# Delta rule with a cosine router: the triangular inverse in 16-row blocks, with a level of matrix products between two blocks

## The chip, the core and the metric

The kernel runs on one core of a Trainium2 chip. The metric is the device time of one execution in microseconds (us). The core has a TensorE for matrix products (PE in the profile, its weight loads PEld), a VectorE (DVE), a ScalarE (ACT), a GpSimd (POOL), and a SyncE (SP) from whose queue most transfers start. Each engine works through its own queue in order and waits for others by semaphores. Matrix products land in PSUM, from which DVE or ACT take them to SBUF.

## What is computed

Two stages, all in fp32. The first is a delta rule over 4 x 8 = 32 heads, 768 steps, head width 48:

```python
B, H, S, D = q.shape                       # 4, 8, 768, 48
k_n = k / (np.linalg.norm(k, axis=-1, keepdims=True) + 1e-06)
state = np.zeros((B, H, D, D), dtype=np.float32)
for t in range(S):
    kt, vt, bt = (k_n[:, :, t], v[:, :, t], beta[:, :, t, None])
    y[:, :, t] = np.einsum('bhd,bhde->bhe', q[:, :, t], state)
    v_old = np.einsum('bhde,bhd->bhe', state, kt)
    state = state + bt[:, :, :, None] * np.einsum('bhd,bhe->bhde', kt, vt - v_old)
```

The second takes y as 3072 tokens of 384 numbers, normalizes them, scores them against 8 experts, sends each token to its best expert (384 to 1024 to 384 with a relu between), and scales the result by the router's probability.

## The kernel before

The delta rule is done in chunks of C = 64 steps. Inside a chunk the steps depend on one another through a unit lower triangular 64 x 64 matrix for each head, which has to be inverted; between chunks only the 48 x 48 state is carried. The kernel has 12 chunks (index m) and splits the 32 heads in two halves (index i), so there are 24 **units**, n = 2m + i. The 128 partitions hold two batches' chunks of 64 steps.

**Groups.** Two chunks (four units) make a group g, six groups in all. `prepare(g)` (L429 to L585) makes what all four units need: it loads k (`planned_k`), forms norms (`square`, `total`, `roots`, `scales`), the scaled keys K (`keys`), turns them on TensorE (`transposes`, L316) and copies them out to KQ on ScalarE. `gram_diag` (L522) then multiplies keys with keys on TensorE for the two 32-row diagonal blocks of each 64 x 64 matrix. `to_lanes` (L553) is a VectorE transpose that brings all those 32 x 32 blocks into lanes: each of the 128 partitions then holds one whole block of 32 x 32 numbers (32 heads x 2 chunks x 2 blocks), in the 128 x 1024 tile X. `lower` (L558, L560, GpSimd) clears what is not below the diagonal.

**Substitution.** The loop of L563 inverts the 32 x 32 block in every partition at once on VectorE: for each j from 1 to 30 a `product` (L568) of a column and a row, (31 - j) x j numbers, and a `subtract` (L572) of it from the rows below. That is 60 dependent VectorE instructions a group. `from_lanes` (L580) transposes the result back to WT, and two ScalarE copies, `spread` (L584, in the trace L283 with W as output), write it into W: for every head a 64 x 64 matrix with the two inverted 32 x 32 diagonal blocks.

**Units.** `unit(n)` (L633) is the recurrence. For one unit: `old` (the state times the keys), `rest` (L677, VectorE, R = V minus that), `solve` (W times R), `y_out` (ScalarE), `fix` (the lower left 32 x 32 corner, Sx), `u_out`, `solve_again` (W again), `z_out`, `update`, `new_state` (L726, or L728 for the first chunk; VectorE). Two such chains, i = 0 and i = 1, run side by side. Each TensorE step is 16 matrix products of 48 to 64 rows and columns, which the trace shows as 32 rows (a fp32 product here is two rows). Beside the chain each unit needs `gram` (keys with keys and queries), `scores` (L659, M), `from_state`, `inside`, the output x and its transposes and router scores; `routing` for every four units; and values and queries are loaded, scaled and turned. `solve` of the first unit of a group cannot start before that group's W.

**Order.** The instructions of the whole first stage are recorded as tasks with an engine, an estimated cost and a due time (`plan.add`), and `Plan.order` lays them out once, before the launch, by a list schedule: of the tasks that are ready by its estimates an engine takes the one with the earliest due time. A due time is written relative to t0, the start of the group or unit, where a unit is given PERIOD = 7.5. The engines then follow that fixed order, whatever the true durations are. PSUM is four pairs of banks; a task with `take` needs a free pair, which its last reader releases.

Tiles X, WT and the k ring lie in the space of the first expert's weights (`w1_first`, `w2_first`), so the trace calls X, WT and the loaded k `w_first`. The weights are loaded there once they are no longer used. `early_tile` does two expert tiles beside the last units. Then comes the second stage (L1115 to L1362): lists of tokens, gathers, and products with 24 loads of 1.5 MB of weights.

## Time and profile before

| | us |
|---|---|
| median of 3 runs | 620.38 (618.40 to 622.43) |
| the profiled execution | 617.46 |
| its span, first to last instruction | 615.6 |
| first stage: first `solve` starts (PE, reads W) | 66.71 |
| first stage: last unit's `rest` (L677) | 315.53 |

In the profile a row of an engine is one instruction: start, duration, engine, line, operation, output and inputs, their shapes, and in brackets how long the engine was idle before it and which event ended that. "issue" means that nothing in the profile explains the wait. A table by windows gives the busy time of each engine in a stretch, with its count of instructions, and PEclk, the clock that TensorE was granted as a share of full speed. TensorE's rows overlap, and their ends are modelled.

The page's first part gives the engines' totals over the span: PE 516.1 us (84%), PEld 425.9, DVE 275.9 (45%), ACT 185.4, POOL 168.5. The 45% of VectorE is an average over two stages: of its 275.9 us, 224.9 lie in the first 300.

### The profile page before, as it was taken

Reading aid. Unit: us, or ns where it says so; the run is one execution under the profiler, and the core shown is the slowest. Engines: PE = TensorE matmul, PEld = TensorE weight load, DVE = VectorE, ACT = ScalarE, POOL = GpSimd, SP = SyncE. Lnnn points to the kernel's source line nnn. Section 1 sums busy time; section 2 is a strip of 40 time slices with the busy share of each in tenths; the row PEclk is TensorE's granted clock in tenths of the full one; section 3 lists DMA queues with packets and bytes.
Section 4 is the critical chain, followed back from the end, with each engine's and each line's share of the span. In section 5 each row is a group of like instructions: output and inputs, shape, how many; then the busy total and the mean of one; then the engine's idle time right before and its main releaser. Section 6 shows DMA issues by size and latency. Waiting matters only on the chain. (4 is left out here: it accounts for less than half of the span.)

```text
span 615.6 us, 21947 instructions
## 1 busy us (share of the span) xinstructions
PE 516.1 (84%) x9643; PEld 425.9 (69%) x9643; DVE 275.9 (45%) x778; ACT 185.4 (30%) x343; POOL 168.5 (27%) x228
## 2 busy tenths in 40 slices
PE   3573688688797878888899599999999999999990
PEld 3462577578686767777887577887767777777870
DVE  4798777777789877962325121111011221121000
ACT  2331534634635536555442020111001221110110
POOL 4433426064534132230212212331202211111100
PEclk9965678667879897998899799999999999999996
DMA  4444734543341340032201599997637666679300
GB/s 81 75 82 82 198 72 71 105 99 70 65 100 32 90 135 18 19 101 66 85 31 43 184 383 384 382 370 256 227 139 245 187 207 237 209 254 338 131 15 18
DMA packets 116334, 90.55 MB, mean 147 GB/s; under 512 B 83394, under 2 KB 105308, under 8 KB 116226
## 3 DMA queue, kind: packets, MB, share of 16 engines
q1 hardware_dynamic: 110722, 77.76, 42.7%
q0 software_dynamic: 4416, 11.06, 5.1%
q8 instruction: 80, 1.31, 0.9%
q10 hardware_dynamic: 1088, 0.20, 0.2%
q14 instruction: 28, 0.23, 0.1%
HBM read 77.06 MB, written 12.13 MB: 145 GB/s over the span
## 5 line engine op out<-in xcount | busy, mean ns | idle before, releaser
L1200 PEld LDWEIGHTS acc<-xTm,w 128*128 128x128 f32 x576 | 77.7, 191 | 5.8 <-issue 1.8
L1202 ACT ACTIVATE hT<-acc 128x512 f32<-128x512 f32 (+3 forms) x52 | 28.5, 548 | 175.2 <-PE acc L1200 175.2
L1200 PE MATMUL acc<-xTm,w 128*128 128x128 f32 (+3 forms) x576 | 80.3, 299 | 0.0
L1217 PE MATMUL acc<-w,hT 128*128 128x384 f32 (+2 forms) x272 | 78.9, 489 | 0.0
L572 DVE TENSOR_TENSOR w_first<-w_first,tmp 128x30 f32<-128x30 f32 (+9 forms) x180 | 69.0, 385 | 3.9
L568 DVE TENSOR_TENSOR tmp<-w_first 128x30 f32<-128x30 f32 (+9 forms) x180 | 66.7, 372 | 4.1
L280 PE MATMUL psum_pair<-KQ 48*32 48x64 f32 (+2 forms) x2304 | 50.0, 265 | 18.9 <-issue 9.2
L1230 POOL DMA_INDIRECT out_dram<-y,more_ids x22 | 21.7, 986 | 160.5 <-DVE y L1220 127.4
L1217 PEld LDWEIGHTS acc<-w,hT 128*128 128x128 f32 (+2 forms) x272 | 42.2, 176 | 30.3 <-issue 5.8
L1191 DVE COPY xTm<-acc 128x384 f32<-128x384 f32 (+3 forms) x26 | 12.6, 508 | 109.1 <-PE acc L1190 104.5
L280 PEld LDWEIGHTS psum_pair<-KQ 48*32 48x32 f32 (+1 forms) x2304 | 42.4, 135 | 24.4 <-issue 12.1
L1220 DVE TENSOR_SCALAR y<-acc,xg 128x384 f32<-128x384 f32 x20 | 12.4, 618 | 97.7 <-PE acc L1217 93.2
L1200 PEld LDWEIGHTS acc<-xTm,w_first 128*128 128x128 f32 x288 | 44.6, 200 | 3.7 <-DVE y L1227 0.6
L1200 PE MATMUL acc<-xTm,w_first 128*128 128x128 f32 (+3 forms) x288 | 46.8, 325 | 0.4 <-DVE xTm L1191 0.4
L1217 PE MATMUL acc<-w_first,hT 128*128 128x384 f32 (+2 forms) x176 | 44.2, 489 | 0.0
L280 PE MATMUL psum_pair<-S,KQ 48*64 48x64 f32 x1408 | 35.6, 244 | 9.9 <-issue 4.7
L280 PEld LDWEIGHTS psum_pair<-S,KQ 48*64 48x64 f32 x1408 | 30.5, 155 | 13.4 <-issue 6.3
L283 ACT ACTIVATE KQ<-psum_pair 128x1024 f32<-128x1024 f32 x24 | 24.4, 1022 | 43.5 <-PE psum_pair L316 33.7
L973 POOL DMA_INDIRECT idmap<-tokid,slots_i x24 | 24.1, 1005 | 42.3 <-DVE slots_i L949 22.8
L1217 PEld LDWEIGHTS acc<-w_first,hT 128*128 128x128 f32 (+2 forms) x176 | 23.1, 163 | 17.8 <-issue 4.5
L622 POOL TENSOR_TENSOR V<-v,sqb 128x384 f32<-128x384 f32 x24 | 20.9, 876 | 48.8 <-DVE R L677 22.0
L469 POOL TENSOR_TENSOR rt<-rn,half 128x32 f32<-128x32 f32 x4 | 22.0, 5488 | 30.2 <-DVE rn L454 30.2
(207 smaller groups left out, 766.2 us busy)
## 6 DMA issues: line engine op xcount, KB each, us to landing
w<-in_moe_w_dram SPq DMA_DIRECT2D x24, 1536.0 KB
w_first<-in_moe_w_dram SPq DMA_DIRECT2D x10, 1536.0 KB
q<-in_q_dram SPq DMA_DIRECT2D x96, 48.0 KB
v<-in_v_dram SPq DMA_DIRECT2D x48, 96.0 KB
w_first<-in_k_dram SPq DMA_DIRECT2D x88, 48.0 KB
x_dram<-XC SPq DMA_DIRECT2D x5, 800.0 KB
idmap<-space SPq DMA_DIRECT2D x1, 2048.0 KB
w_first<-in_moe_w_dram SPq DMA_DIRECT2D x6, 256.0 KB
```

Source lines behind the costliest of these rows:

```text
L280: nc.tensor.matmul(out_, lhsT=lhsT, rhs=rhs, start=start, stop=True, skip_group_check=True)
L283: nc.scalar.activation(out_, in_, ACT.Copy, scale=scale)
L469: nc.gpsimd.tensor_tensor(out=flat(rt, part), in0=flat(ss, part), in1=half[:, 0:w], op=ALU.pow)
L568: nc.vector.tensor_tensor(t, X[:, j + 1:, j:j + 1].broadcast_to([128, rows, j]), X[:, j:j + 1, 0:j].broadcast_to([128, rows, j]), op=ALU.mult)
L572: nc.vector.tensor_tensor(X[:, j + 1:, 0:j], X[:, j + 1:, 0:j], t, op=ALU.subtract)
L622: nc.gpsimd.tensor_tensor(buf("V", m)[:, i * 2 * NP * D:(i + 1) * 2 * NP * D].rearrange("p (jj j d) -> p jj j d", jj=2, d=D), buf("v", m)[ ...
L973: put = nc.gpsimd.indirect_dma_start(out=idmap[:, :], out_offset=bass.IndirectOffsetOnAxis(ap=slot_i[:, i:i + 1], axis=0), in_=K["tokid"][ ...
L1191: nc.vector.tensor_copy(t.xT[:, :, b * T:b * T + n], psX[:, :, 0:n])
L1200: nc.tensor.matmul(psH[:, i, :], lhsT=t.w1[:, j, (f + i) * 128:(f + i + 1) * 128], rhs=t.xT[:, j, 0:t.width], start=(j == 0), stop=(j == K ...
L1202: nc.scalar.activation(t.hT[:, f:f + k, 0:t.width], psH, ACT.Relu)
L1217: nc.tensor.matmul(psO[c:c + w, :], lhsT=t.hT[:, f, b * T + o:b * T + o + w], rhs=t.w2[:, f, :], start=(f < q), stop=(f >= NF - q))
L1230: nc.gpsimd.indirect_dma_start(out=out[:, :], out_offset=bass.IndirectOffsetOnAxis(ap=t.ids[b][0:n, 1:2], axis=0), in_=y[0:n, :], in_offse ...
```

## The change

Substitution now inverts 16 x 16 blocks instead of 32 x 32 ones. The 32 x 32 block of a partition is taken as two 16-row blocks (`blocks`, index e), which go through the loop side by side in the same instructions: j from 1 to 14, 28 instructions a group, each over 2 x (15 - j) x j numbers.

What connects the two 16-row blocks is then made by a **level** of products on TensorE. `rows_from_lanes` transposes the inverted first 16 rows (128 x 512) into WN, `from_lanes` clears one 16 x 16 corner (a memset on VectorE) and transposes the whole X to WT as before. Two ScalarE copies (`rows_spread`, 128 x 512 each, with the new masks `first` and `second`) write WN into W. `level_one` multiplies, for each of 32 places and both halves of the partitions, a 64 x 64 weight out of W with 16 columns of WT: 64 products, in two tasks. `level_one_out` (ScalarE, 128 x 512, mask `lo`) takes that to WN; `level_two` multiplies again, 64 products in two tasks; `merged` (VectorE, 128 x 512) adds the result into WT. Only then come the two `spread` copies of 128 x 1024 that were there before. The level holds one PSUM pair from its first product to `merged`.

All due times of the preparation are two units later (the k load -12 instead of -14 periods, and so on down to -5.4 instead of -7.2 for `gram_diag`); the level's own due time is L1 = -3.3 periods, where W had -1.8 before. X has one buffer instead of two, and W is cleared once at the start (GpSimd memsets of 128 x 2048, two of them). Nothing outside the first stage's preparation is edited; but as the schedule is laid out anew, the order of the instructions around it changes too.

```diff
--- before
+++ after
 HC = 32
+LC = 16
...
-    rings["X"], rings["WT"] = carved(2, [HC, HC], w2_flat), carved(3, [HC, HC], w2_flat)[2:]
-    buffers("tmp", 2, [(HC // 2) * (HC // 2)])
+    lanes = HC * HC + HC
+    rings["X"] = [w2_flat[:, 0:lanes]]
+    rings["WT"] = carved(1, [HC, HC], w2_flat[:, lanes:])
+    rings["WN"] = carved(1, [LC, HC], w2_flat[:, lanes + HC * HC:])
+    buffers("tmp", 2, [2 * (LC // 2) * (LC // 2)])
     buffers("W", 2, [HC, C])
...
+        nc.vector.tensor_scalar_mul(const("second", [128, 1]), nsec, -1.0)
+        nc.vector.tensor_scalar_mul(const("first", [128, 1]), K["nfirst"], -1.0)
+        sub = const("sub", [128, 1], I32)
+        nc.vector.tensor_single_scalar(sub, prow[:, 0:1], HC - 1, op=ALU.bitwise_and)
+        lo = const("lo", [128, 1])
+        nc.vector.tensor_copy(lo, sub)
+        nc.vector.tensor_single_scalar(lo, lo, float(LC), op=ALU.is_lt)
         for t in rings["Sx"]:
             nc.gpsimd.memset(t[:, :, 0:HC], 0.0)
+        for t in rings["W"]:
+            nc.gpsimd.memset(t, 0.0)
...
-            planned_k(m, t0 - 14 * PERIOD + (m % 2) * 2 * PERIOD if m > 1 else -200.0 + 0.5 * m)
+            planned_k(m, t0 - 12 * PERIOD + (m % 2) * 2 * PERIOD if m > 1 else -200.0 + 0.5 * m)
...
-        X = buf("X", g)
+        lane = buf("X", g)
+        X = lane[:, 0:HC * HC].rearrange("p (a b) -> p a b", a=HC)
+        blocks = lane.rearrange("p (e q) -> p e q", e=2)[:, :, 0:LC * HC].rearrange("p e (a b) -> p e a b", b=HC)
 
         def to_lanes():
             nc.vector.transpose(X, pair(("diag", g)).rearrange("p jj (x c) -> p c jj x", c=HC))
-        plan.add(*dve(1024), t0 - 6.5 * PERIOD, to_lanes, hold=g == 0, reads=[("psum", ("diag", g))],
+        plan.add(*dve(1024), t0 - 4.9 * PERIOD, to_lanes, hold=g == 0, reads=[("psum", ("diag", g))],
                  writes=[at("X", g), ("X_next", g % 2)])
 
         def lower():
             nc.gpsimd.affine_select(out=X, in_=X, compare_op=ALU.is_ge, fill=0.0, base=-1,
                                     pattern=[[1, HC], [-1, HC]], channel_multiplier=0)
-            nc.gpsimd.memset(X.rearrange("p a b -> p (a b)")[:, ::HC + 1], -1.0)
-        plan.add("POOL", 1.2, 0.1, t0 - 6.4 * PERIOD, lower, writes=[at("X", g)])
-
-        for j in range(1, HC - 1):
-            rows = HC - 1 - j
-            t = buf("tmp", j)[:, 0:rows * j].rearrange("p (a b) -> p a b", b=j)
+            nc.gpsimd.memset(lane[:, 0:HC * HC:HC + 1], -1.0)
+        plan.add("POOL", 1.2, 0.1, t0 - 4.8 * PERIOD, lower, writes=[at("X", g)])
+
+        for j in range(1, LC - 1):
+            rows = LC - 1 - j
+            t = buf("tmp", j)[:, 0:2 * rows * j].rearrange("p (e a b) -> p e a b", e=2, b=j)
 
             def product(j=j, rows=rows, t=t):
-                nc.vector.tensor_tensor(t, X[:, j + 1:, j:j + 1].broadcast_to([128, rows, j]),
-                                        X[:, j:j + 1, 0:j].broadcast_to([128, rows, j]), op=ALU.mult)
+                nc.vector.tensor_tensor(t, blocks[:, :, j + 1:LC, j:j + 1].broadcast_to([128, 2, rows, j]),
+                                        blocks[:, :, j:j + 1, 0:j].broadcast_to([128, 2, rows, j]), op=ALU.mult)
 
             def subtract(j=j, rows=rows, t=t):
-                nc.vector.tensor_tensor(X[:, j + 1:, 0:j], X[:, j + 1:, 0:j], t, op=ALU.subtract)
-            key = t0 - (6.0 - j * 4.0 / HC) * PERIOD
-            plan.add("DVE", rows * j / 960 + 0.085, 0.13, key, product, reads=[at("X", g)], writes=[at("tmp", j)], hold=g == 0)
-            plan.add("DVE", rows * j / 960 + 0.085, 0.13, key + 0.01, subtract, reads=[at("tmp", j)], writes=[at("X", g)], hold=g == 0)
-
-        WT, W = buf("WT", g), buf("W", g)
+                to = blocks[:, :, j + 1:LC, 0:j]
+                nc.vector.tensor_tensor(to, to, t, op=ALU.subtract)
+            key = t0 - (4.6 - j * 1.2 / LC) * PERIOD
+            plan.add("DVE", 2 * rows * j / 960 + 0.15, 0.1, key, product, reads=[at("X", g)], writes=[at("tmp", j)], hold=g == 0)
+            plan.add("DVE", 2 * rows * j / 960 + 0.15, 0.1, key + 0.01, subtract, reads=[at("tmp", j)], writes=[at("X", g)], hold=g == 0)
+
+        WT, WN, W = buf("WT", g), buf("WN", g), buf("W", g)
+        level = ("level", g)
+        L1 = t0 - 3.3 * PERIOD
+
+        def rows_from_lanes():
+            nc.vector.transpose(WN, X.rearrange("p a b -> p b a")[:, 0:LC])
 
         def from_lanes():
+            nc.vector.memset(X[:, LC:, 0:LC], 0.0)
             nc.vector.transpose(WT, X)
-        plan.add(*dve(1024), t0 - 1.9 * PERIOD, from_lanes, reads=[at("X", g)], writes=[at("WT", g), ("X_next", g % 2)])
+        plan.add(*dve(512), L1, rows_from_lanes, hold=g == 0, reads=[at("X", g)], writes=[at("WN", g)])
+        plan.add("DVE", 1.35, 0.17, L1 + 0.01, from_lanes, hold=g == 0, writes=[at("X", g), at("WT", g), ("X_next", g % 2)])
+        for b, name in enumerate(("first", "second")):
+            def rows_spread(b=b, name=name):
+                act_copy(W[:, :, b * HC:b * HC + LC], WN.rearrange("p r x -> p x r"), K[name])
+            plan.add(*act(512, True), L1 + 0.02, rows_spread, reads=[at("WN", g), "masks"], writes=[at("W", g) + (b,)])
+        half_x = [[jj * 16 + o * 8 + n for jj in range(2) for n in range(8)] for o in range(2)]
+
+        def level_one(xs):
+            def step():
+                p = pair(level)
+                for x in xs:
+                    for o in range(2):
+                        mm(p[HALF[o], 0, x * LC:(x + 1) * LC], W[HALF[o], x], WT[HALF[o], LC:, x])
+            return step
+
+        def level_one_out():
+            act_copy(WN.rearrange("p r x -> p (r x)"), pair(level)[:, 0], K["lo"])
+
+        def level_two(xs):
+            def step():
+                p, part = pair(level), WN.rearrange("p r x -> p (r x)")
+                for x in xs:
+                    for o in range(2):
+                        mm(p[HALF[o], 1, x * LC:(x + 1) * LC], W[HALF[o], x], part[HALF[o], x * LC:(x + 1) * LC])
+            return step
+
+        def merged():
+            to = WT[:, LC:].rearrange("p c x -> p x c")
+            nc.vector.scalar_tensor_tensor(out=to, in0=pair(level)[:, 1].rearrange("p (x c) -> p x c", c=LC),
+                                           scalar=K["lo"], in1=to, op0=ALU.mult, op1=ALU.add)
+        both = [at("W", g) + (0,), at("W", g) + (1,)]
+        for a in range(2):
+            plan.add(*pe(32, 0.0335), L1 + 0.03 + a * 0.01, level_one(half_x[a]), reads=both + [at("WT", g)],
+                     writes=[("psum", level)] if a else (), take=None if a else level)
+        plan.add(*act(512, True), L1 + 0.05, level_one_out, reads=[("psum", level), "masks"], writes=[at("WN", g)])
+        for a in range(2):
+            plan.add(*pe(32, 0.0335), L1 + 0.06 + a * 0.01, level_two(half_x[a]), reads=both + [at("WN", g)],
+                     writes=[("psum", level)])
+        plan.add(*dve(512), L1 + 0.08, merged, hold=g == 0, reads=[("psum", level), "masks"], writes=[at("WT", g)])
         for b, name in enumerate(("nfirst", "nsecond")):
             def spread(b=b, name=name):
                 act_copy(W[:, :, b * HC:(b + 1) * HC], WT.rearrange("p i x -> p x i"), K[name])
-            plan.add(*act(1024, True), t0 - 1.8 * PERIOD, spread, reads=[at("WT", g), "masks"], writes=[at("W", g) + (b,)])
+            plan.add(*act(1024, True), L1 + 0.1, spread, reads=[at("WT", g), "masks"], writes=[at("W", g) + (b,)])
 
...
-                         writes=["w2_first", ("X", 0), ("X", 1), ("WT", 0)])
+                         writes=["w2_first", ("X", 0), ("WT", 0), ("WN", 0)])
```

## The prediction

> **What bounds the kernel now.** I read the table by windows first, because the page averages two stages.
>
> ```profile
> core 0: us, PE busy (x) PEld busy (x) DVE busy (x) ACT busy (x) POOL busy (x), PEclk, DMA share, GB/s
> 0.00:66.00 66.00, 32.13 (x843) 27.19 (x843) 51.35 (x142) 19.63 (x26) 29.92 (x80) 0.76 0.45 80
> 66.00:134.00 68.00, 54.26 (x1657) 47.68 (x1661) 50.46 (x140) 31.52 (x55) 25.24 (x18) 0.73 0.51 114
> 134.00:250.00 116.00, 94.04 (x3506) 85.17 (x3496) 93.68 (x260) 57.91 (x101) 39.64 (x48) 0.87 0.32 72
> 250.00:275.00 25.00, 21.07 (x792) 19.26 (x785) 21.34 (x69) 11.91 (x27) 7.25 (x11) 1.00 0.15 44
> 275.00:300.00 25.00, 21.27 (x837) 19.36 (x829) 8.06 (x27) 14.79 (x29) 3.15 (x4) 0.93 0.24 79
> ```
>
> Up to 66 us, before any unit runs, VectorE is busy 78% and TensorE half idle. From 66 to 250 both are busy about 80%: VectorE 144 and TensorE 148 of 184 us. Past 275 the substitution is over, VectorE drops to a third, TensorE stays at 85%. So TensorE stands close behind VectorE. ScalarE at about half, the transfers and GpSimd are further off.
>
> Second, the groups of VectorE, for what the substitution costs:
>
> ```profile
> L572 DVE TENSOR_TENSOR w_first<-w_first,tmp 128x30 f32<-128x30 f32 (+9 forms) x180 | 69.0, 385 | 3.9
> L568 DVE TENSOR_TENSOR tmp<-w_first 128x30 f32<-128x30 f32 (+9 forms) x180 | 66.7, 372 | 4.1
> ```
>
> 135.7 us, half of all VectorE work: 22.6 us a group. Third, the timeline, for how it holds the units up (first the start, then units 2, 4, 5 and 23 at their `rest`, and the first products of unit 4):
>
> ```profile
> 32.73 0.13 DVE L568 TENSOR_TENSOR tmp<-w_first 128x30 f32<-128x30 f32 x1
> 60.66 0.19 DVE L572 TENSOR_TENSOR w_first<-w_first,tmp 128x30 f32<-128x30 f32 x1
> 62.64 2.07 ACT L283 ACTIVATE W<-w_first,nfirst 128x1024 f32<-128x1024 f32 x1 [7.14 <-DVE w_first L580]
> 90.28 0.55 DVE L677 TENSOR_TENSOR R<-V,psum_pair 128x384 f32<-128x384 f32 x1 [1.38 <-PE psum_pair L280]
> 110.47 0.54 DVE L677 TENSOR_TENSOR R<-V,psum_pair 128x384 f32<-128x384 f32 x1
> 116.51 1.13 PE L280 MATMUL psum_pair<-R,W 64*64 64x64 f32 x32 [1.96 <-ACT W L283]
> 134.02 0.56 DVE L677 TENSOR_TENSOR R<-V,psum_pair 128x384 f32<-128x384 f32 x1 [0.85 <-PE psum_pair L280]
> 315.53 0.56 DVE L677 TENSOR_TENSOR R<-V,psum_pair 128x384 f32<-128x384 f32 x1 [2.23 <-PE psum_pair L280]
> ```
>
> Group 0's substitution takes 28 us, and the first `solve` follows at 66.71. Unit 4's R is ready at 111.0, but its `solve` waits for group 1's W until 116.5. Units 5 to 23 then take (315.53 - 134.02) / 18 = 10.1 us each. With VectorE nearly free, units 18 to 22 take (302.25 - 269.65) / 4 = 8.15 us each.
>
> **VectorE.** Removed: 60 instructions a group. Added: 28 of 28 to 112 elements. The rows of L568 and L572 with 30, 58, 84 and 108 elements have means of 187 to 373 ns, together 264 ns, so 28 x 0.264 = 7.4 us instead of 22.6. Added too: a transpose of 128x512, half of L580's 1.24 us; a memset of 256 elements, 0.27 us as the one of L336; `merged`, between 0.68 us (L659, as large, also from PSUM) and 1.4 us (a strided copy of 1024 costs ScalarE 2.07 us where a plain one costs 1.02); I take 0.8. Net: 22.6 - 7.4 - 1.7 = 13.5 us a group, 81 us in all.
>
> **ScalarE.** Per group two `rows_spread` at half of 2.07 us and one copy of 128x512, 0.6 us between the rows for 384 (0.49) and 1024 (1.02): 2.7 us a group, 0.7 a unit. At half load there is room, but the chain's Y and U are queued behind the spreads, up to 2 us late once a group.
>
> **TensorE.** 128 products a group, 256 rows. Nearest rows: `solve`, also 64x64 weights, has 32 rows in 0.69 us at clock 1 and in 1.13 at the 0.61 of 108 to 131 us. That makes 5.5 us, or 9.0 cold. `gram_diag` with 128 rows in 1.53 us would make 3.1; the small beta products (142 rows in 5.55 us) 10.0. I take `solve` at full clock, 5.5 us a group or 1.4 us a unit, since the weights are the same and only the columns shrink; the ends are 0.8 and 2.5.
>
> The Trainium skill (TensorEngine Tiling, section Instruction Overhead) speaks against the change: a product with one column takes as long as one with 60, so tiling should not be taken from a dimension that is already small. By proportion to the columns (16 of 64) the level would cost 1.4 us a group, by the rule 5.5. The trace sides with the rule: router scores with 8 columns (6 rows in 0.84 us) cost as much a row as transposes with 128 (8 rows in 1.09).
>
> **The start.** No gain by my walk through the new queues. Substitution starts about 1 us later (GpSimd scales V, 1.62 us, before it clears X). In its middle stands `total` for chunk 3, whose ScalarE square now follows two Sx copies; these were at 38.8 and 40.1, and the first product of `gram` can start a little earlier, after the Q copy at 35.2: the square ends near 39.6, VectorE waits some 2.5 us. 28 instructions later it is 46 us. Transposes 2.2, spreads 2.1: 50. On TensorE, in front of the level, stand q of chunk 1 (its second half landed at 47.98), and between the four parts of the level the K transposes (up to 2 us each) and both `gram_diag` (1.5 to 2.6 each) of group 1: 10 to 15 us with the level. Then `merged`, Sx, and W's 4.1 us: first `solve` at 66 to 71 instead of 66.7. I take +2. The W memsets (4.6 us by the rate of L364) lie in GpSimd's idle time before the first K at 16.8.
>
> **Units 0 to 5.** Here the gain is clearest. Group 1's substitution, spread over 64 to 111 us before, needs a sixth of that; the queue of TensorE has unit 2's `old` ahead of group 2's diagonal products, where it stood behind them, and unit 5's first steps between those of units 4 and 6 rather than behind a whole unit and its routing. VectorE's longest remaining wait is for GpSimd's 5.5 us root, until about 79. From there unit 2's `rest` near 84 (before 90.3), unit 4's `solve` near 104 (116.5), unit 5's `rest` near 109 to 112 (134.0). Gain 22 to 25 us.
>
> **Units 5 to 23.** The pace is bounded by 8.15 + 1.4 = 9.55 us below (VectorE free, the level added) and 10.1 + 1.4 = 11.5 above (TensorE already the bound). What speaks for the middle: from 66 to 318 us TensorE was busy 208 of 252 us, the level adds 27, and 235 of 252 cannot be kept with waits for ScalarE and VectorE in the chain, unless rows get shorter. They can: at clock 1.00 a row cost 21.07 / 792 = 26.6 ns, over the whole stretch 28.5. I take 10.4. The last `rest`: 109 + 18 x 10.4 = 296 instead of 315.5: 19.5 us. (W's lateness: its first reader stands 19 to 30 tasks behind the level's last product in TensorE's queue, a unit and more, so I cost it at nothing; if not, see the second rival.)
>
> The skill on the clock gate (TensorE: Matmul & The Clock Gate, section What's actually happening) says that about 3.4 us of sustained work brings the full clock. The trace agrees only roughly: 0.73 over 66 to 134 us at 80% busy, but 1.00 over 250 to 275 at 84%. Going by the rule, all rows would shrink to the full clock's, and the pace would lie at the lower bound, 9.55.
>
> The second stage begins after the first and is unchanged. **Sum:** 617.5 - 19.5 = 598 us on the profiled execution's own time; that lies 2.9 us below the median of the runs, so 601.
>
> **Rivals.** (1) *VectorE was the only brake* (chance 0.14): pace at the lower bound, 9.55: last `rest` at 281, 34.5 us off, 586. For it: the stretch past 275; against: TensorE at 85% there already. (2) *W late, slower* (0.20): from the last substitution to W it took 6 us (60.85 to 66.65); now seven hand-overs through three queues, 15 us without any waiting (2.2 + 2.1 + 2.8 + 0.6 + 2.8 + 0.8 + 4.1), and the preparation comes two units later. TensorE's queue is in order, so a level that waits for ScalarE holds the units' steps behind it. If W's second half ends after R of the group's first unit, each group pays; at 8 us for five groups, 40 - 19.5 makes 641; the sign turns at about 4 us a group. Against: the place of its first reader. (3) *TensorE is the bound* (0.16): pace 11.5, last `rest` at 109 + 207 = 316: no change, 621. The forecast has 0.50, with its own range 590 to 613.
>
> **Chances.** About 1% (6 us) is what this measurement can tell from no change. Faster by more: nearly all of the forecast, rival 1, a little of the third: 0.64. Slower: rival 2 and a part of the third: 0.22. Same: 0.14. The range of 8 in 10 reaches from a little beyond rival 1 to half of rival 2: 579 to 630.
>
> **What would show it.** VectorE busy near 195 us; 128x512 copies of `rows_spread` near 1.04 us; the level's 64 rows near 1.4 us; first `solve` at 66 to 71; unit 5's `rest` near 110; 10.4 us a unit after it; TensorE over 88% busy from 110 us on. I am wrong if a wait of TensorE for ScalarE's W or WN shows more than 4 us a group, if the level's rows cost more than 30 ns each, or if the time gained by unit 5 is lost again by unit 23.

## The result and the profile after

The change makes the kernel slower: 685.58 us (676.88 to 688.85, four runs) against 621.12 (618.40 to 622.43) on the same chip, a ratio of 1.096 with a 95% interval of 1.090 to 1.103. The ratio counts only executions within 1.5% of the fastest of their kernel, so it is smaller than that of the medians (1.104), and the profiled execution, 688.62 us with a span of 686.9, is not among them; the profiles of prep_early and two_banks below, whose executions do count, show the same price of the level (77.4 and 77.0 us). The forecast was 601, its range 579 to 630.

| start of | before, us | forecast | after |
|---|---|---|---|
| first `solve` | 66.71 | 66 to 71 | 76.28 |
| unit 2's `rest` | 90.28 | 84 | 88.10 |
| unit 5's `rest` | 134.02 | 109 to 112 | 141.91 |
| last `rest` (unit 23) | 315.53 | 296 | 385.20 |
| pace of units 5 to 23, us a unit | 10.1 | 10.4 | 13.5 |

What comes after the last `rest` is as long as before, 686.9 - 385.2 = 301.7 us against 300.1. The whole loss lies in the first stage. Its windows, in the columns of the table before (length, busy time and count for each engine, granted clock, transfers):

```profile
0.00:66.00 66.00, 40.28 (x984) 36.46 (x984) 37.75 (x116) 17.48 (x25) 27.01 (x78) 0.71 0.51 105
66.00:142.00 76.00, 67.88 (x1903) 63.38 (x1904) 33.03 (x96) 36.59 (x59) 24.38 (x22) 0.69 0.33 62
142.00:250.00 108.00, 95.26 (x2955) 88.22 (x2956) 44.71 (x117) 45.67 (x77) 35.15 (x36) 0.73 0.29 62
250.00:300.00 50.00, 44.31 (x1352) 41.33 (x1349) 16.76 (x49) 21.45 (x35) 8.40 (x12) 0.77 0.24 63
300.00:385.00 85.00, 75.02 (x2354) 69.16 (x2358) 30.07 (x110) 37.28 (x80) 18.48 (x26) 0.87 0.17 52
```

VectorE did get lighter: 41% busy between 142 and 250 us, where it was 81% between 134 and 250. TensorE is 88 or 89% busy from 66 us on, and at a lower clock: 0.69 to 0.77 until 300 us, where before had 0.87 to 1.00 from 134 on. What filled it stands on the page in the costliest groups: the level, its products and the weight loads that overlap them (busy us, mean ns of a row):

```profile
L284 PE MATMUL psum_pair<-w_first,W 64*64 64x16 f32 x1536 | 77.1, 250 | 7.4 <-issue 4.2
L284 PEld LDWEIGHTS psum_pair<-w_first,W 64*64 64x64 f32 x1536 | 75.4, 200 | 10.6 <-issue 6.4
```

77.1 us for six groups is 12.85 us a group, 50 ns a row; the prediction had 5.5. The timeline shows two prices:

```profile
46.94 3.60 PE L284 MATMUL psum_pair<-w_first,W 64*64 64x16 f32 x64 [1.70 <-ACT KQ L287]
76.28 1.98 PE L284 MATMUL psum_pair<-V,W 64*64 64x64 f32 x64 [1.33 <-ACT W L287]
92.42 3.44 PE L284 MATMUL psum_pair<-w_first,W 64*64 64x16 f32 x62
141.91 0.55 DVE L738 TENSOR_TENSOR R<-V,psum_pair 128x384 f32<-128x384 f32 x1
213.40 2.04 PE L284 MATMUL psum_pair<-w_first,W 64*64 64x16 f32 x64 [0.29 <-DVE S L787]
385.20 0.56 DVE L738 TENSOR_TENSOR R<-V,psum_pair 128x384 f32<-128x384 f32 x1 [2.58 <-PE psum_pair L284]
```

64 rows take 2.04 us at best and mostly 3.4 to 3.6. `solve`, with four times the columns, has 64 rows in 1.98 us there (the line at 76.28). The longer price goes with a low clock while TensorE has no pause: from 89 to 110 us it was busy 21.00 of 21.00 us, weight loads 20.82, and the granted clock there was 0.51:

```profile
89.00:110.00 21.00, 21.00 (x436) 20.82 (x429) 4.80 (x8) 5.44 (x8) 3.05 (x4) 0.51 0.12 23
```

Last, the waits of TensorE for ScalarE's W (the level's and `solve`'s weights) and for KQ, the costliest for ScalarE (total, times, longest, over the whole span):

```profile
PE psum_pair L284 <- ACT KQ L287: 4.7, 6, 1.7
PE psum_pair L284 <- ACT W L287: 2.3, 2, 1.3
```

2.3 us in two waits for W, and no row of the list has a wait for WN: the second rival, a late W, did not happen. (24 waits, 27.2 us over the whole span, stand as "issue", without a cause in the profile.)

### The profile page after: what moved, and what is told of

The parts are those of the page before. It is cut to its first block, busy times and chain, and to the rows that moved or that the text cites. A ratio compares the mean times of both kernels' runs of the same rounds, so it can differ in the third digit from the quotient of the medians.

```text
span 686.9 us, 24896 instructions
## 1 busy us (share of the span) xinstructions
PE 601.2 (88%) x11179; PEld 510.9 (74%) x11179; DVE 209.3 (30%) x609; ACT 200.5 (29%) x361; POOL 170.2 (25%) x230
## 5 line engine op out<-in xcount | busy, mean ns | idle before, releaser
L284 PE MATMUL psum_pair<-w_first,W 64*64 64x16 f32 x1536 | 77.1, 250 | 7.4 <-issue 4.2
L284 PEld LDWEIGHTS psum_pair<-w_first,W 64*64 64x64 f32 x1536 | 75.4, 200 | 10.6 <-issue 6.4
L1278 PE MATMUL acc<-w,hT 128*128 128x384 f32 (+2 forms) x272 | 81.6, 500 | 0.0
L1263 ACT ACTIVATE hT<-acc 128x512 f32<-128x512 f32 (+3 forms) x52 | 28.5, 548 | 180.0 <-PE acc L1261 179.9
L1278 PEld LDWEIGHTS acc<-w,hT 128*128 128x128 f32 (+2 forms) x272 | 43.6, 181 | 31.7 <-issue 8.3
L284 PE MATMUL psum_pair<-KQ 48*32 48x64 f32 (+2 forms) x2304 | 52.9, 270 | 12.4 <-issue 9.1
L284 PEld LDWEIGHTS psum_pair<-KQ 48*32 48x32 f32 (+1 forms) x2304 | 45.8, 140 | 16.1 <-issue 11.4
L1252 DVE COPY xTm<-acc 128x384 f32<-128x384 f32 (+3 forms) x26 | 12.6, 508 | 109.8 <-PE acc L1251 106.4
L284 PE MATMUL psum_pair<-S,KQ 48*64 48x64 f32 x1408 | 37.5, 250 | 7.5 <-issue 5.0
L1281 DVE TENSOR_SCALAR y<-acc,xg 128x384 f32<-128x384 f32 x20 | 12.4, 618 | 100.3 <-PE acc L1278 95.8
L284 PEld LDWEIGHTS psum_pair<-S,KQ 48*64 48x64 f32 x1408 | 32.6, 161 | 10.2 <-issue 6.4
```

The source lines that it names most:

```text
L284: nc.tensor.matmul(out_, lhsT=lhsT, rhs=rhs, start=start, stop=True, skip_group_check=True)
L1252: nc.vector.tensor_copy(t.xT[:, :, b * T:b * T + n], psX[:, :, 0:n])
L1263: nc.scalar.activation(t.hT[:, f:f + k, 0:t.width], psH, ACT.Relu)
L1278: nc.tensor.matmul(psO[c:c + w, :], lhsT=t.hT[:, f, b * T + o:b * T + o + w], rhs=t.w2[:, f, :], start=(f < q), stop=(f >= NF - q))
L1281: nc.vector.tensor_scalar_mul(y, psO, t.x[b][:, Dm:Dm + 1])
```

## The experiments

The theory after this profile: the level's own time on TensorE is the loss, and the time freed on VectorE brings nothing, since VectorE did not set the pace. Rivals: the later due times, the level's hand-overs, the shared PSUM bank, the strided operand. Of the last the profile itself disposes: `level_one` reads a strided moving operand and `level_two` a plain one, and both have 3.4 to 3.6 us for 64 rows in group 1 (starts 92 to 109 us).

Where a kernel leaves work out, the tokens go to other experts and the second stage changes, so the start of the last `rest` is compared. It is one number from one profile, and the first stage differs from chip to chip: the same kernel (the tiny substitution below) had 331.6 on one chip and 316.3 on another, and the kernel before took 635.4 and 627.3 on these two chips, one execution each (its profiled execution on the second, before_again, took 620.0, so two executions on one chip can be 7 us apart too). So between chips some 15 us decide nothing; the table names the time of the kernel before on each chip, a median of 3 or more executions except for 635.4 and 627.3.

| kernel | before there | level on TensorE, us | unit 5 | last `rest` | pace |
|---|---|---|---|---|---|
| before, first profile | 621.1 | 0 | 134.0 | 315.5 | 10.1 |
| after | 621.1 | 77.1 | 141.9 | 385.2 | 13.5 |
| prep_early | 620.0 | 77.4 | 161.3 | 386.6 | 12.5 |
| two_banks | 620.0 | 77.0 | 141.3 | 392.1 | 13.9 |
| quads_banks | 620.0 | 40.5 | 128.1 | 354.0 | 12.6 |
| no_level | 620.0 | 0 | 113.4 | 325.6 | 11.8 |
| before_late | 621.5 | 0 | 118.1 | 324.2 | 11.5 |
| no_level_early | 621.5 | 0 | 109.1 | 313.0 | 11.3 |
| no_level_nospread | 621.5 | 0 | 114.3 | 314.1 | 11.1 |
| quads_wide | 621.5 | 33.4 | 129.3 | 354.2 | 12.5 |
| sub_tiny | 635.4 | 0 | 134.8 | 331.6 | 10.9 |
| level_quarter | 635.4 | 18.2 | 120.9 | 343.5 | 12.4 |
| diag_wide | 635.4 | 55.3 | 134.9 | 379.2 | 13.6 |
| before_again | 627.3 | 0 | 134.7 | 318.1 | 10.2 |
| sub_tiny_again | 627.3 | 0 | 133.0 | 316.3 | 10.2 |
| sub_tiny_planned | 627.3 | 0 | 106.6 | 305.4 | 11.0 |
| fewer_products | 627.3 | 0 | 134.7 | 319.9 | 10.3 |
| extra_products | 635.5 | 77.4 (added) | 168.8 | 396.6 | 12.7 |
| both_lighter | 635.5 | 0 | 132.3 | 320.0 | 10.4 |

### The level left out

```diff
-        for a in range(2):
-            plan.add(*pe(32, 0.0335), L1 + 0.03 + a * 0.01, level_one(half_x[a]), ...)
...
-        plan.add(*dve(512), L1 + 0.08, merged, hold=g == 0, ...)
```

> The changed kernel without the level: both tasks of level_one and of level_two, level_one_out and merged are left out, so the block between two 16-row blocks is missing from the result; substitution, transposes, spreads and due times stay. Theory A (the level's products on TensorE are the loss: 77 us of TensorE time, 61 of them beside units, at half the clock): the time falls by 60 us or more against the changed kernel, below the kernel before: 580 to 610 us. Theory B (the later due times or the new order are the loss): it stays above 650.

Unit 5 comes at 113.4, about where the forecast had it with the level, and the last `rest` at 325.6: without the level some 60 us of the stage are gone. (Its total, 764.22 us, would by the letter speak for theory B, and decides nothing: with the tokens at other experts, what comes after the last `rest` takes 436.8 us instead of 300.) But it is no earlier than in the kernel before, whose 315.5 it misses by 10. The stretch in between (113 to 326), and the last `rest`:

```profile
113.00:326.00 213.00, 175.02 (x5805) 161.25 (x5806) 93.59 (x293) 107.32 (x198) 71.94 (x80) 0.81 0.30 71
325.62 0.56 DVE L729 TENSOR_TENSOR R<-V,psum_pair 128x384 f32<-128x384 f32 x1 [1.24 <-PE psum_pair L284]
```

VectorE is at 44%, with no level on TensorE, and a unit takes 11.8 us. Two trials more, with the earlier due times, and without the copies of the rows (`rows_from_lanes`, `rows_spread`) that only the level needs:

```diff
-        plan.add(*dve(512), L1, rows_from_lanes, ...)
...
-            plan.add(*act(512, True), L1 + 0.02, rows_spread, ...)
```

> The changed kernel without the level (as in no_level) and with all due times two units earlier; the block between two 16-row blocks is missing from the result, so tokens go to other experts and only the first stage's time counts: the start of the last unit's rest. Theory A: 320 to 330 us, as with the later due times. Theory B: 305 us or less.

> The changed kernel without the level and without rows_from_lanes and the two rows_spread copies that feed it (2.4 us of ScalarE a group), late due times kept; the same block is missing from the result, only the first stage counts. If those copies, which stand before the chain's own in ScalarE's queue, are the 10 us: last rest at 316 us or less. If they only fill idle time: 322 to 330 us.

313.0 and 314.1. The first lies between its two expectations; the second is what the copies as the cause had asked for, but the earlier due times alone gave as much, and both differences lie within what two chips can differ. The change without its level stands level with the kernel before, within what profiles of one execution can tell. The gain at the start, 20 to 25 us at unit 5, is there each time, and each time units 5 to 23 give it back.

### The due times

```diff
-        L1 = t0 - 3.3 * PERIOD
+        L1 = t0 - 4.9 * PERIOD
...
-            plan.add(*pe(64, 0.02), t0 - 5.4 * PERIOD, gram_diag(m), ...)
+            plan.add(*pe(64, 0.02), t0 - 7.2 * PERIOD, gram_diag(m), ...)
```

> The changed kernel with all due times of the preparation two units earlier again (the level's at -4.9 periods). Theory A (the level's products cost TensorE time wherever they stand): within 1.5% of the changed kernel, 670 to 695 us. Theory B (late preparation makes the units wait for W): 640 us or less.

> The kernel before with the preparation's due times as the change has them, two units later up to the clearing of X, and the substitution's from -4.6 to -2.0 periods; nothing else changed. Theory A (the due times cost nothing, TensorE sets the pace): within 1% of the kernel before, 614 to 627 us. Theory B (the later preparation is why the changed kernel without its level still ends its first stage at 325.6 us, 10 us behind the kernel before, though VectorE has 75 us less to do): 630 us or more.

The changed kernel with all due times of before: 688.9 us, ratio 1.109 (1.100 to 1.119), no better. The kernel before with the later due times: 623.7 us, ratio 1.004 (1.001 to 1.007). So the later preparation costs next to nothing. It does move the start: unit 5 came at 118 instead of 134 with the old substitution and as much work on VectorE as ever (228.8 us up to its last `rest`, before 228.6), and that too was lost again by unit 23 (324.2).

### What makes the level's rows long

Three edits of the level alone. The halves' products into two PSUM banks instead of one; then in addition the products rotated over all four 64 x 64 quadrants of TensorE, as `solve` has them (the level uses the two diagonal ones); then 64 columns instead of 16 (another head's numbers, so the block between is left out). The fourth line has the 64 columns on the change's own two quadrants. `level_two` is edited likewise.

```diff
-                        mm(p[HALF[o], 0, ...], W[HALF[o], x], WT[HALF[o], LC:, x])
+                        mm(p[HALF[o], o, ...], W[HALF[o], x], WT[HALF[o], LC:, x])              # two_banks
+                        mm(p[HALF[o ^ x % 2], o, ...], W[HALF[o], x], WT[HALF[o], LC:, x])      # quads_banks
+                        mm(p[HALF[o ^ x % 2], o, ...], W[HALF[o], x], W[HALF[o], (x + 1) % HC]) # quads_wide
+                        mm(p[HALF[o], 0, ...], W[HALF[o], x], W[HALF[o], (x + 1) % HC])         # diag_wide
```

> The level's products of the two partition halves write two PSUM banks, as solve's do, instead of one (the copy and the merge take two instructions each). If the shared bank is what makes 64 rows of the level take 2.04 us (full clock) to 3.60 us: they fall to about 1.4 to 2.3 us, and the time to 640 us or less. If not: rows as before, and the time within 1.5% of the changed kernel's.

> As with two banks, and every second product of the level writes the other partition half, so that its products go round all four 64x64 quadrants of the array in solve's order (half of the level's results stand on the wrong partitions). If it is the two quadrants alone, each loaded again and again, that make the level's rows slow: 64 rows in 1.4 us (full clock) to 2.3 us, and the time 620 to 650 us. If 16 columns behind a 64x64 weight cost so much in themselves: rows of 32 to 56 ns as before, and about 680 us.

> As quads_banks, but each product of the level takes 64 columns (of W) instead of 16, written over one another in the same bank; the level's results mean nothing, only the first stage counts (354.0 us with 16 columns, granted clock 0.50 during the level). If it is the few columns that let the clock fall, the level runs at a clock of 0.9 or more, 64 rows take about 1.2 to 1.4 us instead of 1.9, and the last rest comes at 350 us or earlier although the level streams four times as much. If the columns do not matter to the clock: 64 rows take 2.2 to 2.5 us cold, and the last rest comes at 360 us or later.

> The changed kernel with 64 columns instead of 16 in each of the level's products, on the same two quadrants and in the same bank; the columns are another's data, so the block between is left out and the total cannot be compared; the first stage can. Theory (products of 16 columns let the granted clock fall, and products of 64 keep it): 64 rows take 2.0 to 2.4 us nearly everywhere instead of mostly 3.4 to 3.6, and the last rest comes 10 to 30 us earlier than 385. Rival (the two quadrants alone set the price): 64 rows take 3.4 us or more in the early groups as before, and the last rest stays within 6 us of 385.

The level's group in the four profiles, in this order:

```profile
L284 PE MATMUL psum_pair<-w_first,W 64*64 64x16 f32 x1536 | 77.0, 249 | 7.4 <-issue 3.0 <-ACT KQ L287 1.9 <-ACT W L287 1.6
```

```profile
L284 PE MATMUL psum_pair<-w_first,W 64*64 64x16 f32 x1536 | 40.5, 246 | 9.8 <-issue 6.3 <-ACT KQ L287 1.9 <-ACT W L287 1.4
```

```profile
L284 PE MATMUL psum_pair<-W 64*64 64x64 f32 x1536 | 33.4, 236 | 13.8 <-issue 10.3 <-ACT KQ L287 1.9 <-ACT W L287 0.9
```

```profile
L284 PE MATMUL psum_pair<-W 64*64 64x64 f32 x1536 | 55.3, 231 | 9.6 <-issue 5.3 <-ACT W L287 2.0 <-ACT KQ L287 1.7
```

The mean of one row hardly moves (231 to 250 ns): rows overlap, and what changes is how many are under way at once. So the busy time of the group is read, not the mean. The bank is nothing (77.0; the kernel took 691.77 us). The quadrants halve the price: 40.5, 64 rows in 1.12 us at best and 1.85 to 1.91 at a low clock. That kernel took 655.03 us, ratio 1.052 (1.043 to 1.060), a little beyond the 620 to 650 expected; half of its results lie on other partitions, so the inverse it uses is not that of the change, but what comes after its last `rest` is as long as before (302.2 us). The columns count the wrong way round: with 64 of them the same number of rows takes less time, 33.4 instead of 40.5 on four quadrants and 55.3 instead of 77.0 on two, because the clock stays up (64 rows in 2.0 to 2.1 us nearly everywhere on two quadrants). Group 1's level in the change and in diag_wide, then a part of diag_wide's level at a low clock (0.50 from 47 to 52 us):

```profile
92.00:109.00 17.00, 17.00 (x370) 16.87 (x366) 1.55 (x3) 3.17 (x7) 0.05 (x1) 0.50 0.08 15
```

```profile
92.00:102.00 10.00, 9.60 (x353) 9.27 (x354) 1.50 (x2) 2.96 (x6) 0.00 (x0) 1.00 0.23 43
47.73 3.68 PE L284 MATMUL psum_pair<-W 64*64 64x64 f32 x64 [1.71 <-ACT KQ L287]
```

At the same clock the columns make next to no difference: 3.68 us for 64 rows against 3.60 with 16 columns at the low one, 2.08 against 2.04 at the high one. So the difference between 77.0 and 55.3 lies in how long the clock was low. For diag_wide the price of the rows came as the theory had it; the stage's end, 379.2, is 6 us earlier on a chip that was slower, and decides nothing. For quads_wide too the price came as expected (64 rows mostly in 1.16 us, a granted clock of 0.90 from 86 to 97 us), but the stage's end did not: 354.2 where 350 or earlier was expected, as late as quads_banks with 7 us more of level.

### A quarter of the level

```diff
-                for x in xs:
+                for x in xs[:8:2] if xs[0] == 0 else xs[1:8:2]:
```

> The changed kernel with its order of work and hand-overs kept, but only 32 products a group in the level (16 in each step) instead of 128, of 64 columns, on the same two quadrants, the halves into two banks. The other products of the block between are left out, so the result differs and the total cannot be compared; the first stage can. Theory (the level's TensorE time is the loss): at about 1 us for each 32 products the level takes 1 to 2 us a group instead of 12.9, and the last rest comes at 325 to 335, as without the level (325.6). Rival (the level's hand-overs, that is the copies, the merge and TensorE's waits for them, are the loss): 345 or later.

The level took 18.2 us, 3.0 a group where 1 to 2 were expected, and the last `rest` came at 343.5, between the two expectations, on the chip where the kernel with the tiny substitution had 331.6. What the hand-overs cost by themselves this run does not separate.

### Is VectorE the brake, or TensorE?

First the kernel before with a substitution of one element an instruction, its order kept: on a chip without a profile of the kernel before, then beside one.

```diff
-                nc.vector.tensor_tensor(X[:, j + 1:, 0:j], X[:, j + 1:, 0:j], t, op=ALU.subtract)
+                nc.vector.tensor_tensor(X[:, j + 1:j + 2, 0:1], X[:, j + 1:j + 2, 0:1], t[:, 0:1, 0:1], op=ALU.subtract)
```

> The kernel before, with every product and subtraction of the substitution cut to one element: the number, order and hand-overs of VectorE's instructions stay, their elements go. The inversion is thereby left out, so what follows selects other keys, and the total cannot be compared; the first stage can. VectorE gets some 70 to 100 us lighter before the last rest (135.7 us of substitution in before, about 60 instructions a group of some 80 to 130 ns left). Theory (from the third unit on TensorE and the chain of the state set the pace, and VectorE only the start): units 5 to 23 keep 9.5 to 10.1 us each, unit 5's rest starts 15 to 25 us earlier than 134, and the last rest by no more than that plus about 10, at 285 to 300. Rival (VectorE was the brake all through, as the prediction had it): the pace falls to about 8.2 us and the last rest to 255 to 270. If the pace gets longer than 10.1 as it did without the level, then a lighter VectorE by itself brings the units closer and makes something else late, and the start's gain is lost again.

The first, sub_tiny, fits none of its expectations: unit 5 came at 134.8 and not 15 to 25 us earlier, the pace was 10.9, the last `rest` came at 331.6, on a chip where the kernel before took 635.4. So it was repeated beside a profile of the kernel before.

> The kernel before, unchanged, for a profile on the same chip as the three trials beside it. Expected: the last rest within 8 us of the first profile's 315.5, the pace of units 5 to 23 at 9.9 to 10.4 us, TensorE some 83% busy and VectorE some 70% busy in that stretch.

> The substitution cut to one element an instruction, order kept, the inversion left out, so only the first stage can be compared. Theory (TensorE's products set the pace): the last rest stays within 8 us of before_again's. Rival (VectorE's work sets the pace): with some 35 us less of it between unit 5 and unit 23 the last rest comes 25 us or more earlier.

The windows from unit 5 to unit 18 (135 to 272 us), where the substitution is, of the kernel before and of this one on the same chip (for the kernel before also the stretch up to its last `rest`, for a later trial), with the last `rest` of each:

```profile
135.00:272.00 137.00, 110.65 (x4129) 100.86 (x4130) 109.73 (x315) 66.76 (x122) 46.31 (x58) 0.86 0.30 68
...
135.00:318.00 183.00, 150.79 (x5476) 137.55 (x5478) 125.80 (x373) 89.92 (x173) 56.60 (x72) 0.88 0.28 69
318.13 0.55 DVE L677 TENSOR_TENSOR R<-V,psum_pair 128x384 f32<-128x384 f32 x1 [2.23 <-PE psum_pair L280]
```

```profile
135.00:272.00 137.00, 111.38 (x4186) 101.41 (x4175) 74.98 (x313) 66.73 (x125) 44.51 (x56) 0.88 0.29 67
316.25 0.55 DVE L676 TENSOR_TENSOR R<-V,psum_pair 128x384 f32<-128x384 f32 x1 [2.23 <-PE psum_pair L280]
```

VectorE does as many instructions in 75.0 us instead of 109.7, and nothing else moves: unit 18's `rest` at 269.98 against 272.01, the last at 316.3 against 318.1. 35 us of VectorE work were worth 2 us. Then the same with the plan's costs cut, so that the order is made for the small work:

```diff
-            plan.add("DVE", rows * j / 960 + 0.085, 0.13, key, product, ...)
+            plan.add("DVE", 0.09, 0.13, key, product, ...)
```

> The same tiny substitution, with the plan's costs for it cut too (0.09 us for each instruction), so that the order is made for the small work. The inversion is left out; only the first stage can be compared. Theory (TensorE's products set the pace, VectorE only the start): the first solve and unit 5 come 10 us or more earlier than before_again's, units 5 to 23 take 10 us or more each, and the last rest comes at most 12 us earlier. Rival (VectorE is the brake, and the order of the trial beside it hid that): the pace falls below 9.3 us, the last rest comes 25 us or more earlier.

Now the first `solve` starts at 56.4 instead of 66.8 and unit 5's `rest` at 106.6 instead of 134.7: the start is gained by the order made for the short instructions, while the short instructions in the old order gained 2 us there. Units 5 to 23 take 11.0 us each, and 12.8 us are left at the last `rest` (12 at most was expected). With these due times that is about the most a cheaper substitution had to give.

Next TensorE, with VectorE's work unchanged:

```diff
-            four(f)
+            for a, b in CORNERS:
+                f(a, b, 0)
```

> The kernel before with only 4 of the 32 products in each of three steps of a unit (the correction by the corner, the second solve, the scores times the values), from unit 2 on, order and hand-overs kept; the other heads' parts are left out, so only the first stage can be compared. VectorE's work is unchanged. That takes 3 x 28 products of some 0.24 us, overlapping at about 25 ns each, some 35 to 40 us of busy TensorE from units 5 to 23 (three groups of 576 products, 42.9 us, by 28/32). Theory (TensorE's products set the pace): the last rest comes 25 to 40 us earlier than before_again's and the pace falls to 8.0 to 8.8 us. Rival (VectorE is the brake, at 127 of 182 busy and more): the last rest moves by less than 10 us.

(A step of a unit has 16 products, 32 of the trace's rows, of which 4 products were kept: three quarters of 42.9 us, 32 us, was the time to be saved, not 35 to 40.) The last `rest` did not move: 319.9. Three groups of TensorE between 135 and 318 us, of before_again, then the window from unit 5 on and the same groups of fewer_products:

```profile
L280 PE MATMUL psum_pair<-S,KQ 48*64 48x64 f32 x1140 | 28.5, 243 | 6.9 <-issue 3.7 <-DVE S L726 1.6 <-ACT KQ L283 1.5
...
L280 PE MATMUL psum_pair<-U,W 64*64 64x64 f32 x576 | 15.2, 240 | 3.8 <-issue 1.9 <-ACT U L283 1.8
...
L280 PE MATMUL psum_pair<-R,W 64*64 64x64 f32 x576 | 14.1, 239 | 2.8 <-DVE R L677 2.0 <-issue 0.9
```

```profile
135.00:320.00 185.00, 158.50 (x4200) 142.67 (x4192) 125.24 (x374) 90.72 (x174) 56.10 (x72) 0.70 0.27 67
```

```profile
L280 PE MATMUL psum_pair<-S,KQ 48*64 48x64 f32 x1096 | 31.8, 277 | 3.5 <-DVE S L731 2.4 <-DVE lz L801 0.7
...
L280 PE MATMUL psum_pair<-R,W 64*64 64x64 f32 x576 | 17.5, 275 | 4.9 <-DVE R L677 3.9 <-issue 0.8
...
L280 PE MATMUL psum_pair<-U,W 64*64 64x64 f32 x144 | 7.6, 279 | 2.6 <-ACT U L283 1.6 <-issue 1.0
```

With 1,276 rows fewer TensorE is busy 8 us longer (158.5 against the 150.8 of before_again's window above, which is 2 us shorter). The granted clock fell from 0.88 to 0.70, and the rows that stayed got longer (R,W from 14.1 to 17.5 us for the same 576). The three cut groups fell from 42.9 to 21.4 us (7.6, 7.0 and 6.8), not to a quarter; the rest of TensorE's work grew from 107.9 to 137.1, a factor of 1.27, and the clock alone (0.88 / 0.70) gives 1.26. By the letter the expectation's rival came true, but VectorE as the brake is what sub_tiny_again speaks against. TensorE's busy share is thus no measure of its load: the work that was taken out came back as a lower clock. Both cuts together:

> The kernel before with the substitution cut to one element an instruction and with 4 of the 16 products of three steps of a unit from unit 2 on (the two trials of the batch before, together), order and hand-overs kept; the inversion and the other heads' parts are left out, so only the first stage can be compared. Each alone left the last rest where it was (316.3 and 319.9 against 318.1). If VectorE and TensorE take turns as the brake, both together bring it 15 us or more earlier, to 303 or less. If the chain of hand-overs in the written order, or a clock that falls as TensorE gets less to do, holds the pace, it stays within 8 us of 318.

320.0, at a clock of 0.72. The edit is that of the two trials above. On this chip the kernel before was again at 635.5, with no profile, so up to some 15 us of gain cannot be excluded, and which of hand-overs and clock holds the pace of the kernel before stays open.

### The level's work without the level

The reverse, and the plainest test of the theory: the kernel before, with as many products as the level has, of the same 16 columns on the same two quadrants (their weights are 48 x 64). No instruction reads what they make; but a group's diagonal products, and with them its substitution, stand behind them in TensorE's queue.

```diff
+                for x in range(32):
+                    for o in range(2):
+                        lhs = KQ[o * C:o * C + D, x // 16, x // 4 % 4, x // 2 % 2]
+                        mm(p[HALF[o], 0, m % 2 * 256:m % 2 * 256 + 16], lhs[:, 0:C], lhs[:, 0:16])
                 for step in range(2 * NP):
```

> The kernel before, with 128 more products a group of 16 columns on two quadrants, written ahead of the diagonal blocks' products into the space that these fill next, so nothing depends on them and the result is that of before. That is the level's amount of TensorE work, 256 of the trace's rows a group, without the level's copies, merge and waits, in the order of before. At 32 to 56 ns a row it is 8 to 14 us a group, some 40 to 70 us for the five groups that lie beside units. Theory (the level's loss is TensorE's time): the last rest comes 35 to 65 us later than 315 to 318, and the whole kernel by as much. Rival (the loss lies in the level's place ahead of the inverse W, or in its hand-overs): 20 us later or less.

```profile
L280 PE MATMUL psum_pair<-KQ 48*64 48x16 f32 x1536 | 77.4, 252 | 0.8 <-issue 0.7
396.64 0.55 DVE L681 TENSOR_TENSOR R<-V,psum_pair 128x384 f32<-128x384 f32 x1 [3.25 <-ACT XC L283]
```

The same 77 us, and the same loss: 699.02 us against 635.49, ratio 1.101 (1.093 to 1.109), where the change has 1.096 (1.090 to 1.103). The last `rest` is at 396.6, 79 us behind before_again's; against the chip's own kernel before the loss is 63.5 us. No copy, merge or wait of the level is in this kernel, and VectorE's substitution is all there. So the products alone make a loss of this size, and within these intervals all the rest of the change together comes to about nothing in the total. Stretch by stretch it does not: up to unit 5 the added products cost 34 us (168.8 against 134.7) and the change 8, from there on 44 and 62. The change gains at the start, by its order, and loses that again.

No version here beats the kernel before: with the level on four quadrants, the best form of it that was timed in several executions, it is still 1.052 times as long.

## Why the prediction was wrong, step by step

**The level on TensorE** is the step that failed. It was taken at "`solve` at full clock, 5.5 us a group", with a cold end of 9.0 and a far one of 10.0. Measured: 12.85, beyond every end; 6 x 7.35 = 44 us in all above the term. Of the 89 us by which the last `rest` missed the forecast (385.2 against 296), 33 stood at unit 5 already; without the level 30 were left (325.6), and those are the second step's. The nearest row was chosen by the weights' size. What it hid are two things that the row of `solve` shows only to one who asks where its products lie: `solve` rotates over four quadrants and the level over two (77.0 against 40.5 us), and its 64 columns keep the clock up where 16 do not (77.0 against 55.3).

The rule weighed there, of the Trainium skill (TensorEngine Tiling, section Instruction Overhead), that a product of one column takes as long as one of 60, pointed the right way, against the change, but it too gave 5.5. At one and the same clock the runs agree with it for these sizes: 16 columns took as long as 64 (3.60 and 3.68 us for 64 rows). What it has no term for is that with 16 the clock was low for longer, which made the level 1.2 to 1.4 times as long as with 64. The rule on the clock (TensorE: Matmul & The Clock Gate, section What's actually happening), full clock after some 3.4 us of sustained work, does not hold here: 21 us without a pause in the profile, at 0.51.

**The pace with VectorE free, 8.15 us**, is the second failed step. It was read from units 18 to 22, where the substitution had ended, and put down to the free VectorE. But the kernel with a light VectorE has 10.5 us a unit from unit 5 to unit 18, (269.98 - 132.98) / 13, as the kernel before on that chip has 10.6. What else differs in units 18 to 22 is the preparation, gone from all engines, and the clock (0.93 to 1.00); which of them shortens these units is not shown. So the gain in units 5 to 23 had no ground: without the level they took 11.1 to 11.8 us, not 9.0 (10.4 less the level's 1.4).

**VectorE's saving** was sized nearly right. The substitution took (24.2 + 25.1) / 6 = 8.2 us a group (taken: 7.4), the strided `merged` 1.12 (0.8), VectorE in all 209.3 us (195). It saved 66.6 us (of the 81 forecast), and no run with the change's substitution shows a gain in the last `rest` beyond what two chips can differ; the most that a lighter substitution brought by itself were the 12.8 us of sub_tiny_planned. **ScalarE**: `rows_spread` 1.21 and 1.17 us (1.04), the copy 0.69 (0.6).

**The start.** The 109 to 112 us for unit 5 were forecast with the level and met only without it (109 to 114), so that the number was met there is chance; of its reasons the order in the queues holds (before_late has 118.1 with the old substitution). With the level, group 0's four parts took 3.6 us each, the level with the work between its parts 23.5 us (46.9 to 70.4) where 10 to 15 were allowed, and the first `solve` came at 76.3, without the level at 51 to 54; group 1's level filled 92 to 109 us; unit 5 came at 141.9.

**The rivals.** VectorE as the only brake: refuted. W late: TensorE waited 2.3 us for it. TensorE as the bound: the mechanism that came nearest. With the measured price its sum, the old pace and the level on top, is 10.1 + 77.1 / 24 = 13.3 us a unit (12.8 with the 48.2 us of level that ran after unit 5, over 18 units), and 13.5 was measured. The row of 28.5 ns that the forecast weighed for 66 to 318 us is 28.8 (207.8 us for 7,206 rows); nothing hangs on it. Of the three signs of error that the prediction named, two came true, rows over 30 ns (50), and the gain at unit 5 lost again by unit 23 (in the kernels without the level); the wait for ScalarE did not.

**Open**: what holds the pace of the kernel before. Added products cost about their time (63.5 to 79 us for 77.4); products removed gained nothing.

## What to carry to other kernels

When work moves to TensorE as many small products, price it by a row that agrees in the quadrants it uses and in its columns, not in the weights alone, and put the price of a low clock at the upper end. An engine that is 80% busy beside another at 80% is not thereby a brake: before work is moved off it, make its instructions tiny with the order kept, and see whether anything moves. A gain at the start of a pipeline counts only as far as it is still there at its end.

## What the hardware showed unexpectedly

- Products of 16 columns on two quadrants ran at a granted clock of 0.51 for 21 us in which TensorE had no pause (its weight loads were busy for 20.82). With 64 columns as many rows took 55.3 instead of 77.0 us, all by the clock: at a low clock 64 rows took 3.60 and 3.68 us, at a high one 2.04 and 2.08.
- Two of the four 64 x 64 quadrants: 2.04 us for 64 rows at best, four: 1.12.
- With nearly a quarter of its rows gone (1,276 of 5,476) TensorE was busy longer (158.5 us against 150.8) at a clock of 0.70 instead of 0.88.
- The first stage of one and the same kernel differed by 15 us between one execution on each of two chips (331.6 and 316.3 at the last `rest`), while the rest of the span was as long (342.1 and 341.9 us).
